# First 256 columns of two FFN weights loaded as f32 by the SyncE queue and rounded on chip, in a fused sparse-attention and GEGLU kernel

## The chip, the cores and the metric

One core of one Trainium2 chip. The metric is the device time of one execution in microseconds (us), the median of several runs. One run of the kernel before that took 1450.72 us is slow and left out. In the clock records of the traces here TensorE's granted clock is 1.00 or 0.50; each run's mean grant is given beside its time.

## The reference, cut to what matters

```python
def _attn_ref(q, k, v):                      # (4, 8, 768, 64)
    k_sum = k.reshape(B, H, nb, 32, D).max(axis=3)      # block maxima of keys
    v_sum = v.reshape(B, H, nb, 32, D).mean(axis=3)     # block means of values
    ...                                       # band of +-15 keys, and all block summaries
    return np.matmul(a, v_all)

def _moe_ref(x, w_gate, w_val, w_out, w_res):           # x (3072, 512), d_ff 1536
    g = x @ w_gate
    gelu = 0.5 * g * (1.0 + erf(g * inv_sqrt2))
    ffn_out = gelu * (x @ w_val) @ w_out
    res_gate = 1.0 / (1.0 + np.exp(-(x @ w_res)))
    return x + res_gate * ffn_out
```

All inputs are f32 in HBM; the kernel multiplies in bf16.

## The kernel before

The work is cut into eight units of 384 tokens. The attention of unit 0 has nothing to hide under; from then on the attention of unit n+1 lies between the FFN matmuls of unit n. All loads that turn f32 into bf16 go through the Pool queue, in this order: keys, queries, the twelve tiles of V, then both FFN weights in six chunks of 256 columns.

```python
v_loads(0, 0, 6)                   # V, 64 KB a tile as bf16, by the Pool queue
...                                # masks
v_loads(0, 6, NT)
...
for c in range(6):                 # 256 KB each as bf16, cast in flight
    sl = slice(c * 256, (c + 1) * 256)
    nc.gpsimd.dma_start(out=w_gate[:, :, sl], in_=wg_src[:, :, sl])
    nc.gpsimd.dma_start(out=w_val[:, :, sl], in_=wv_src[:, :, sl])
    if c == 4:
        q_sb[1] = load_q(1, QJ)
# then w_res, the rims of V, w_out, the next batch
```

The start of unit 0, where the change puts its load and its roundings (cuts marked):

```python
k_step(0, 3, ps_mm, "mm")          # last keys: turn, place, block maxima on VectorE
keep_warm(5)                       # matmuls for nothing, for TensorE's clock (see e3_warm)
...                                # queries, scores
nc.vector.tensor_copy(x[QT:BAND, 1:HT, :, 0:D], ...)        # vext copy 1
nc.vector.tensor_copy(x[QT:QT + WIN, 0:HT, :, 0:D], ...)    # vext copy 2
vsum_mm(0, vs, 0, 3)               # block means of V, tile by tile, on TensorE
...
vsum_mm(0, vs, 5, NT)              # needs V's last tile
nc.vector.tensor_copy(vblk[96:128, 0:H // 2, 0:D], ...)
nc.scalar.copy(vblk[96:128, H // 2:H, 0:D], ...)
nc.scalar.activation(gate1[:], bias_t[0:1, :], AF.Gelu)     # loads Gelu's table, 1.28 us
for hp in range(4):
    av_first(hp, st, ao[hp], 0, BAND)
...
for hp in range(4):
    av_first(hp, st, ao[hp], BAND, 128)
    av_end(hp, st, ao[hp])         # reciprocal and product on VectorE
...                                # turn x, then g and vv of the first unit
```

Names in the profile: `vext` is V with its rims, `vs` the block means of V as TensorE sums them and `vblk` the same as bf16; `ao` is attention's output, `xn` the same divided, `xT` it turned for the FFN; `g` and `vv` are the products with w_gate and w_val, `wp` the target of the warming matmuls, `w` the f32 tile w32.

The softmax here doesn't subtract the row's maximum and nothing guards it: scores larger than these inputs give would overflow.

## Time and profile before

| | kernel before |
|---|---|
| median of the timed runs, us | 260.91 (260.88 to 261.61) |
| the profiled run, us, and its span | 262.43, 260.5 |
| TensorE busy | 96% |
| V's last tile: issue, landing, us | 13.32, 16.2 |
| its sums on TensorE end, us | 17.76 |
| first reciprocal, first FFN matmul, us | 19.31, 21.33 |
| last chunk of w_val lands, us | 39.04 |

The lines of the page, the chain, the waits and the stretches stand in the prediction below. Here are TensorE's time line around V's last sums (start, length, operation, count), and V's last load.

```profile
16.06 1.70 PE L246 MATMUL vs<-vext,bmat 64*32 64x256 bf16 x14
17.69 0.95 PE L328 MATMUL ao<-vext,P 96*64 96x65 bf16 x48
...
19.78 0.82 PE L436 MATMUL wp<-warm 128*128 128x512 bf16 x3
```

```profile
L103 POOL DMA_DIRECT2D vext<-in_v_dram x1: 722/722/722, 13.3 to 13.3; - x1
...
DMA to landing us min/median/max: 2.9/2.9/2.9
```

No bracket stands behind the first two lines of TensorE, so it does not wait there: V's last tile is in place 1.2 us before its turn.

### The profile page before, as it was taken

Reading aid. Unit: us, or ns where it says so; the run is one execution under the profiler, and the core shown is the slowest. Engines: PE = TensorE matmul, PEld = TensorE weight load, DVE = VectorE, ACT = ScalarE, POOL = GpSimd, SP = SyncE. Lnnn points to the kernel's source line nnn. Section 1 sums busy time; section 2 is a strip of 40 time slices with the busy share of each in tenths; the row PEclk is TensorE's granted clock in tenths of the full one; section 3 lists DMA queues with packets and bytes.
Section 4 is the critical chain, followed back from the end, with each engine's and each line's share of the span. In section 5 each row is a group of like instructions: output and inputs, shape, how many; then the busy total and the mean of one; then the engine's idle time right before and its main releaser. Section 6 shows DMA issues by size and latency. Waiting matters only on the chain.

```text
span 260.5 us, 5798 instructions
## 1 busy us (share of the span) xinstructions
PE 251.3 (96%) x2294; PEld 138.1 (53%) x2294; DVE 156.1 (60%) x344; ACT 126.3 (48%) x210; POOL 104.5 (40%) x142
## 2 busy tenths in 40 slices
PE   6999889999999999999999999999999999999993
PEld 2565444555555565545654565545654565556543
DVE  5945562579657644577858544778666544854424
ACT  6685337557373435623383437443493338253320
POOL 8896345266080689045250898064530000000000
PEclk9999999999999999999999999999999999999999
DMA  5999999999962899949912999959903500230002
GB/s 82 177 123 174 197 214 203 196 118 193 79 121 47 145 161 123 143 117 156 133 40 56 179 131 137 113 128 164 154 4 85 140 0 3 48 137 0 0 20 103
DMA packets 98155, 29.61 MB, mean 114 GB/s; under 512 B 83368, under 2 KB 94960, under 8 KB 98016
## 3 DMA queue, kind: packets, MB, share of 16 engines
q0 software_dynamic: 68400, 14.96, 69.0%
q1 hardware_dynamic: 29728, 14.29, 25.0%
q8 instruction: 18, 0.29, 0.5%
q14 instruction: 9, 0.07, 0.1%
HBM read 29.36 MB, written 6.29 MB: 137 GB/s over the span
## 4 chain that ended last, share of the span: by engine, by line
PE 82%; DMA 11%; POOL 3%; ACT 1%; issue 1%; DVE 1%; POOLq 0%
PE f L404 23%; PE g L356 22%; PE vv L356 22%; PE r L394 8%; DMA w_val<-in_moe_w_val_dram 5%; DMA w_gate<-in_moe_w_gate_dram 3%; DMA q_sb<-in_q_dram 3%; PE ao L316 3%; PE s L280 2%; POOL vext L103 1%; PE f L428 1%; PE vs L254 1%; PE tp L205 1%; POOL w_val L190 1%; POOL w_gate L189 1%
## 5 line engine op out<-in xcount | busy, mean ns | idle before, releaser
L362 DVE TENSOR_TENSOR gvT<-ge,vv 128x384 bf16<-128x384 f32 x96 | 52.9, 553 | 53.4 <-PE vv L356 48.5
L361 ACT ACTIVATE ge<-g 128x384 f32<-128x384 f32 x96 | 46.9, 490 | 73.5 <-DVE gvT L362 43.5
L356 PE MATMUL vv<-xT,w_val 128*128 128x384 bf16 x384 | 78.8, 326 | 1.3 <-DMA w_val<-in_moe_w_val_dram 1.3
L356 PE MATMUL g<-xT,w_gate 128*128 128x384 bf16 x384 | 78.8, 326 | 0.2
L404 PE MATMUL f<-w_out,gvT 128*128 128x512 bf16 x276 | 64.9, 380 | 0.0
L356 PEld LDWEIGHTS <-w_val 128*128 128x128 bf16 x384 | 37.3, 98 | 27.0 <-DMA w_val<-in_moe_w_val_dram 2.8
L356 PEld LDWEIGHTS <-w_gate 128*128 128x128 bf16 x384 | 36.7, 98 | 26.1 <-issue 1.6
L404 PEld LDWEIGHTS <-gvT 128*128 128x128 bf16 x276 | 25.7, 98 | 29.4 <-issue 0.3
L103 POOL DMA_DIRECT2D vext<-in_v_dram x48 | 32.6, 716 | 13.2 <-DMA w_out<-in_moe_w_out_dram 4.8
L397 ACT ACTIVATE th<-r 128x512 f32<-128x512 f32 x24 | 13.6, 604 | 28.4 <-PE r L394 28.4
L266 POOL COPY vext<-vsum 32x1536 bf16<-32x1536 bf16 x12 | 17.1, 1463 | 23.2 <-DMA vsum<-vpart 23.2
L410 DVE SCALAR_TENSOR_TENSOR th<-th,f 128x512 f32<-128x512 f32 (+1 forms) x25 | 16.5, 661 | 15.7 <-PE f L404 15.4
L302 DVE TENSOR_TENSOR P<-P,maskt 128x768 bf16<-128x768 bf16 x28 | 16.2, 581 | 12.6 <-ACT P L298 8.0
L394 PE MATMUL r<-w_res,xT 128*128 128x512 bf16 x96 | 23.2, 380 | 0.0
L336 DVE TENSOR_TENSOR xn<-ao,rz 128x384 bf16<-128x384 f32 x32 | 17.8, 557 | 1.1
L413 DVE SCALAR_TENSOR_TENSOR o<-th,xn 128x512 f32<-128x512 f32 (+1 forms) x25 | 17.3, 691 | 0.9
L298 ACT ACTIVATE P<-s,bias_t 128x768 bf16<-128x768 f32 x17 | 15.3, 901 | 4.7 <-PE s L280 4.5
L117 POOL DMA_DIRECT2D k_nat<-in_k_dram x24 | 16.4, 746 | 0.9 <-DMA k_nat<-in_k_dram 0.5
L123 POOL DMA_DIRECT2D q_nat<-in_q_dram x18 | 15.9, 918 | 0.8 <-issue 0.7
L295 ACT ACTIVATE P<-s,bias_t 128x384 bf16<-128x384 f32 x30 | 15.7, 578 | 0.3 <-PE s L280 0.3
L212 DVE TENSOR_REDUCE ks<-kW 128x24 bf16<-128x768 bf16 x16 | 15.1, 944 | 0.1
L394 PEld LDWEIGHTS <-xT 128*128 128x128 bf16 x96 | 8.8, 98 | 9.9
(85 smaller groups left out, 167.9 us busy)
## 6 DMA issues: line engine op xcount, KB each, us to landing
out_dram<-o SPq DMA_DIRECT2D x23, 256.0 KB, 2.3
vext<-in_v_dram POOLq DMA_DIRECT2D x48, 64.0 KB, 6.4
q_nat<-in_q_dram POOLq DMA_DIRECT2D x18, 128.0 KB, 7.7
w_gate<-in_moe_w_gate_dram POOLq DMA_DIRECT2D x6, 256.0 KB, 9.4
w_val<-in_moe_w_val_dram POOLq DMA_DIRECT2D x6, 256.0 KB, 10.8
w_out<-in_moe_w_out_dram POOLq DMA_DIRECT2D x3, 512.0 KB, 11.7
k_nat<-in_k_dram POOLq DMA_DIRECT2D x24, 64.0 KB, 4.8
vext<-vext SPq DMA_DIRECT2D x6, 144.0 KB, 6.1
```

What stands on the lines that cost most here:

```text
L103: nc.gpsimd.dma_start(out=vext[b % 2][0:QT, t, :, 0:D], in_=v[b, :, t * QT:(t + 1) * QT, :].rearrange("h p d -> p h d"))
L117: nc.gpsimd.dma_start(out=k_nat[:, t].rearrange("p (h d) -> p h d", d=D), in_=k[b, :, t * QT:(t + 1) * QT, :].rearrange("h p d -> p h d"))
L266: eng.tensor_copy(vext[b % 2][96:128, lo:hi, :, 0:D], src)
L302: nc.vector.tensor_mul(Pf, Pf, maskt.unsqueeze(1).to_broadcast([128, 2 * HT, QT]))
L336: nc.vector.tensor_mul(xn, ao[:, :, :, 0:D], rz.to_broadcast([128, NSUB, 2, D]))
L356: nc.tensor.matmul(ps[:, 0:TU], w[:, ko, fo * 128:(fo + 1) * 128], st["xT"][:, ko, :], start=(ko == 0), stop=(ko == KO - 1), skip_group_ch ...
L361: nc.scalar.activation(ge[:], g[:, 0:TU], AF.Gelu)
L362: nc.vector.tensor_mul(gvT[:, fo, :], ge[:], vv[:, 0:TU])
L394: nc.tensor.matmul(r[:], st["xT"][:, ko, ss], w_res[:, ko, :], start=(ko == 0), stop=(ko == KO - 1))
L404: nc.tensor.matmul(st["f", sub][:], gvT[:, fo, ss], w_out[:, fo, :], start=(fo == 0), stop=(fo == FO - 1), skip_group_check=True)
L410: nc.vector.scalar_tensor_tensor(th[:, cs], th[:, cs], 1.0, f[:, 0:n], ALU.add, ALU.mult)
L413: nc.vector.scalar_tensor_tensor(o.rearrange("p (k d) -> p k d", d=128), th[:, cs].rearrange("p (k d) -> p k d", d=128), 0.5, x, ALU.mult, ...
```

## The change

The intent: the first chunks of both weights, with which every unit's FFN begins, no longer queue behind V on the Pool queue. They come by the SyncE queue, as f32 and without the cast that the Pool queue's loads do in flight, and VectorE and ScalarE round them in gaps of their own. The Pool queue has two chunks less to carry. Two memsets of one element make the load wait for VectorE to be through with the last keys' block maxima (in the trace after, the memsets start at 13.5 us and SyncE's first issue at 13.62).

```diff
+        w32 = qk.tile([128, 2, KO, 256], F32, tag="k_nat", name="w32")
...
-        for c in range(6):
+        for c in range(1, 6):
...
         k_step(0, 3, ps_mm, "mm")
+        for i in range(2):
+            nc.vector.memset(w32[0:1, i, 0, 0:1], 0.0)
+        nc.sync.dma_start(out=w32[:, 0], in_=wg_src[:, :, 0:256])
+        nc.sync.dma_start(out=w32[:, 1], in_=wv_src[:, :, 0:256])
         keep_warm(5)
...
+        nc.vector.tensor_copy(w_gate[:, :, 0:256], w32[:, 0])
         nc.scalar.activation(gate1[:], bias_t[0:1, :], AF.Gelu)
+        nc.scalar.copy(w_val[:, :, 0:256], w32[:, 1])
```

More of the change, by code (lines that the diff above doesn't have):

```diff
@@ L154, in own_keys @@
                                          ap=[rows.ap[0], [34, n]]), 1.0 / BLK)
+        w32 = qk.tile([128, 2, KO, 256], F32, tag="k_nat", name="w32")
+        wg_src = moe_w_gate.rearrange("(ko ki) f -> ki ko f", ki=128)
+        wv_src = moe_w_val.rearrange("(ko ki) f -> ki ko f", ki=128)
         nc.vector.memset(warm[:], 0.0)
@@ L182 @@
         nc.vector.memset(vext[1][0:QT, :, :, D + 1:VP], 0.0)
-        wg_src = moe_w_gate.rearrange("(ko ki) f -> ki ko f", ki=128)
-        wv_src = moe_w_val.rearrange("(ko ki) f -> ki ko f", ki=128)
-        for c in range(6):
+        for c in range(1, 6):
             sl = slice(c * 256, (c + 1) * 256)
```

## The prediction

> **What bounds the kernel now.** I read the page first, then the chain of waits in order of time, the waits of TensorE, the time line of each engine between 12 and 46 us, the transfers' landing times tile by tile, and the stretches' DMA rate. The page, by engine, by slice and by chain:
>
> ```profile
> PE 251.3 (96%) x2294; PEld 138.1 (53%) x2294; DVE 156.1 (60%) x344; ACT 126.3 (48%) x210; POOL 104.5 (40%) x142
> ...
> PE   6999889999999999999999999999999999999993
> ...
> PE 82%; DMA 11%; POOL 3%; ACT 1%; issue 1%; DVE 1%; POOLq 0%
> ```
>
> The reader is to see that TensorE is busy 96% of the span, so only some 9 us are not matmul time at all, and that no slice after the opening is empty. DMA owns 11% of the chain (28 us), but that is no gain of 28 us: TensorE works beneath nearly all of it. The chain in order of time says where those 11% lie:
>
> ```profile
> 3.15 7.21 DMA q_sb<-in_q_dram
> ...
> 17.51 8.75 DMA w_gate<-in_moe_w_gate_dram
> 26.54 12.49 DMA w_val<-in_moe_w_val_dram
> 39.09 0.82 PE vv L356 x4
> ```
>
> All before 39.1 us; from there on the chain is TensorE to the end. So the FFN weights' stream paces the first unit, and afterwards nothing but matmul count does. What the pacing costs is seen in TensorE's own waits and its time line:
>
> ```profile
> PE vv L356 <- DMA w_val<-in_moe_w_val_dram: 1.3, 2, 1.2
> PE tp L238 <- DMA q_sb<-in_q_dram: 0.8, 1, 0.8
> PE s L280 <- ACT qT L240: 0.3, 1, 0.3
> ...
> 31.90 0.82 PE L356 MATMUL vv<-xT,w_val 128*128 128x384 bf16 x4 [1.17 <-DMA w_val<-in_moe_w_val_dram]
> ...
> 36.09 0.36 PE L238 MATMUL tp<-ident,q_sb 96*64 96x96 bf16 x8 [0.76 <-DMA q_sb<-in_q_dram]
> ...
> 39.09 0.82 PE L356 MATMUL vv<-xT,w_val 128*128 128x384 bf16 x4 [0.18 <-DMA w_val<-in_moe_w_val_dram]
> ```
>
> Three waits, 1.17 + 0.76 + 0.18 = 2.1 us: about all that any better weight stream can return. The first FFN matmul (21.33 us) does not start late because of a weight: it follows ScalarE's copy of xT (20.80 us). Its partner on w_val waits 0.55 us of weight-load time for a landing at 21.6 us, which is at most 0.3 us more. Now the stream itself, by stretch (DMA share and GB/s as written are the last two numbers):
>
> ```profile
> 13.00:14.00 1.00, 1.00 (x19) 0.71 (x18) 0.93 (x5) 1.00 (x3) 1.00 (x3) 1.00 2.00 123
> 14.00:15.00 1.00, 1.00 (x18) 0.52 (x17) 0.97 (x2) 1.00 (x4) 1.00 (x3) 1.00 1.60 101
> 15.00:16.00 1.00, 1.00 (x18) 0.45 (x16) 0.75 (x1) 0.82 (x1) 1.00 (x1) 1.00 1.54 84
> 16.00:17.00 1.00, 1.00 (x19) 0.82 (x12) 0.00 (x0) 0.83 (x2) 1.00 (x3) 1.00 0.87 68
> 17.00:18.00 1.00, 1.00 (x26) 0.72 (x26) 0.31 (x1) 0.42 (x2) 1.00 (x2) 1.00 1.35 180
> ...
> 19.00:20.00 1.00, 1.00 (x49) 0.84 (x48) 0.66 (x2) 0.67 (x2) 1.00 (x3) 1.00 0.86 109
> ...
> 25.00:26.00 1.00, 1.00 (x8) 0.61 (x7) 0.67 (x2) 0.48 (x2) 0.76 (x1) 1.00 1.46 197
> ```
>
> From 22 to 36 us the stream holds 196 to 200 GB/s of bf16 written, i.e. 392 to 400 GB/s of f32 read, and I take that as its ceiling. Between 14 and 22 us it is below it, worst at 16 to 17 us: V has landed (last issue 13.3 us, 2.9 us to landing, so 16.2 us), while the first weight DMA, whose issue ends at 15.0 us, only begins to move. That hole is what the change aims at.
>
> [...] No run yet shows a SyncE load beside the Pool stream; the trace's 200 GB/s ceiling is what I hold it to. [...] the two first weight issues take 1.01 and 1.07 us beside VectorE's two copies into vext (13.62 to 15.75 us), the later ones 0.74 to 0.80 us. [...] No f32 copy within SBUF is in this trace. [...] 478 ns for 384 elements and 798 ns for 768, 0.83 ns each.
>
> **The change, part by part.**
> Removed: two 256 KB casting DMAs of the Pool queue, one of each weight. Everything behind them moves up two places. At the ceiling, 256 KB written takes 262 KB / 197 GB/s = 1.33 us, so the Pool stream would be 2.7 us ahead if the other queue cost it nothing.
> Added on DMA: the same f32 bytes on the SyncE queue, 2 x 524 KB. HBM reads stay at 29.36 MB. At 394 GB/s read they need 2.7 us of the ceiling as well. So the stream gains only as far as they fill time that was unused. Unused from 14.5 to 17.5 us, in bf16-equivalents: V's packets (128 B) run at up to 609 per half microsecond and weight packets (512 B) at 192, counted from the trace's records in half microseconds; scaled so, about 520 of the 1024 weight packets fit, 1.35 us. The dip of 19 to 22 us holds up to another 380 packets, 1.0 us, if it can be filled. Stream gain: 1.4 to 2.3 us.
> When they land: VectorE ends the last key's rims at 13.59 us, two memsets of 0.06 us follow, so SyncE issues at about 13.75 and 14.35 us (its issues last 0.34 to 0.62 us, and the stores' packets start some 0.75 us after an issue begins). Alone 1.35 us each; shared with V's tail and from 16.5 us with the Pool stream: w_gate lands at about 17 us, w_val at about 18.5 to 19.3 us (estimate).
> Added on VectorE: the rounding of 1024 elements a partition. [...] It sits behind the vblk cast (ends 18.12 us) and ahead of the first reciprocal (19.31 us), which waits 1.19 us for TensorE. It fits. The memsets' 0.13 us push the vext copies, behind which TensorE does not wait.
> Added on ScalarE: 1024 elements, 798 + 256 x 0.833 = 1.01 us. It sits behind the Gelu table's load and its dummy (end 19.68 us) and ahead of the first xT copy (20.80 us), idle for 1.12 us. It fits, with 0.1 us to spare, if w_val has landed by 19.7 us.
>
> What TensorE gets: the waits at 31.90, 36.09 and 39.09 us go if the stream leads by 1.2, 1.9 and 2.1 us. The next thing due, the first third of w_out (issued 33.0 us, 11.6 us to landing, needed at 44.69 us), has no slack now and must come 2 us earlier too. So TensorE's gain is the smaller of the stream's gain and some 2.2 us: 1.4 to 2.2, centre 1.8 us. TensorE is full from there, so it is carried to the end: 260.9 - 1.8 = 259.1 us, 0.7%.
>
> **The rivals.**
> A. The SyncE load lands late. Both roundings stand in in-order queues ahead of the softmax division and the xT copies, so each late microsecond delays the first FFN matmul by as much. For: before, w_val's first chunk landed 6.6 us after its issue at 15.0. Against: 1 us of margin on VectorE, the empty DMA time at 16 us, and a quicker queue. One microsecond late would leave the gain at about 1.2 us (the weights ahead would still have been the bound): 259.7 us. Two late: 260.6 us.
> B. The load delays V. V's last tiles land at 16.2 us, their sums need the last at about 17.4 us; small V packets that take turns with 1 KB packets could eat that 1.2 us. Then the vblk cast, attention and all behind slip by up to 1 us: 260 us.
> C. The bandwidth is only moved: the Pool stream loses to the SyncE queue what it gained, its dips stay, and the waits stay in another place. 260.9 us, no change.
> D. All waits go and the start is earlier by 0.3 us: 258.4 us.
>
> **Range and chances.** I give the main line 55%, A or B in part 25%, C 12%, D 8%. Range 258.3 to 260.7 us. The 2% mark is 5.2 us; the waits that can be removed are 2.4 us, and a loss of 5 us would need the load to land near 25 us. Faster 1%, within 2% 98%, slower 1%.
>
> **What will show it.** Right: no DMA idle above 0.3 us before the matmuls on w_val and the second q transposes; w_gate's f32 landing before 18.1 us and w_val's before 19.7 us; the first reciprocal still at 19.3 us, the first FFN matmul at 21.2 to 21.4 us; the stretch of 16 to 17 us above 150 GB/s; the matmuls behind the first unit some 1.8 us earlier, the rest of the trace shifted and unchanged. Wrong: VectorE or ScalarE idle on w32 (A); TensorE waiting for vext at 16 to 18 us (B); the last w_val still landing near 39 us (C).

## The result, and the profile after

The changed kernel took 263.65 us (262.72 to 264.48, four runs) beside 260.89 us of the kernel before: ratio 1.0101, 95% interval 1.0052 to 1.0149. Ratios are the mean time of one kernel's fast runs over that of the other's of the same rounds, so not quite the ratio of the medians. The runs fall into two pairs: 262.72 and 262.91 us at a mean clock of 0.992, 264.40 and 264.48 us at 0.987 and 0.986. The profile is of the run of 262.91 us. Its page:

```profile
span 261.0 us, 5804 instructions
...
PE 252.3 (97%) x2294; PEld 139.1 (53%) x2294; DVE 156.1 (60%) x347; ACT 127.3 (49%) x211; POOL 103.0 (39%) x140
...
PEclk9997999999999999999999999999999999999999
...
PE 89%; DMA 5%; POOL 2%; ACT 2%; DVE 1%; issue 0%; POOLq 0%
```

The reader is to see a contradiction: DMA's share of the chain fell from 11 to 5%, as was intended, TensorE is busier than before, and the run is longer. The one 7 in the row of the clock is the hint. TensorE's waits from 15 to 46 us and its time line give the rest:

```profile
PE vs L247 <- DMA vext<-in_v_dram: 1.5, 1, 1.5
PE s L281 <- ACT qT L241: 0.3, 1, 0.3
```

```profile
16.02 1.48 PE L247 MATMUL vs<-vext,bmat 64*32 64x256 bf16 x12
19.02 0.37 PE L247 MATMUL vs<-vext,bmat 64*32 64x256 bf16 x2 [1.51 <-DMA vext<-in_v_dram]
...
21.41 1.46 PE L437 MATMUL wp<-warm 128*128 128x512 bf16 x3
...
23.76 0.50 PE L357 MATMUL g<-xT,w_gate 128*128 128x384 bf16 x1
```

All waits for w_val and q_sb are gone. In their place stands a new one: the sums over V's last tile break off after 12 of 14 matmuls and wait 1.51 us. Then the three warming matmuls take 1.46 us in place of 0.82: TensorE runs at half clock. V's last load, issued at the same time as before, and the stretches around it (columns: length; busy us and instructions of PE, PEld, DVE, ACT, POOL; granted clock, DMA share, GB/s):

```profile
L103 POOL DMA_DIRECT2D vext<-in_v_dram x1: 722/722/722, 13.3 to 13.3; - x1
...
DMA to landing us min/median/max: 5.7/5.7/5.7
```

```profile
15.00:16.00 1.00, 1.00 (x18) 0.44 (x15) 0.73 (x1) 0.78 (x1) 1.00 (x1) 1.00 0.72 72
...
18.00:19.00 1.00, 0.00 (x0) 0.00 (x0) 0.00 (x0) 0.00 (x0) 1.00 (x3) 1.00 1.11 367
...
22.00:23.00 1.00, 1.00 (x7) 0.49 (x5) 0.96 (x3) 0.24 (x1) 0.33 (x1) 0.50 1.45 196
```

V's last tile lands 5.7 us after its issue, at 18.97 us, in place of 2.9. In the microsecond from 18 to 19 three engines do nothing at all, while the DMA engines move 367 GB/s. The granted clock is at 0.50 from 21.36 to 24.77 us, 3.41 us. What the DMA engines are busy with, in half a microsecond from 18.0 us (queue: packets, MB, share; q1 is SyncE's, q0 Pool's):

```profile
q1 hardware_dynamic: 179, 0.18, 103.4%
q0 software_dynamic: 17, 0.00, 6.0%
```

These 17 are the last of V's packets. The slowing began 3 us earlier: in the half microsecond from 15.0 us the Pool queue moved 402 packets in the kernel before, and here, with the load hardly begun:

```profile
q0 software_dynamic: 161, 0.02, 62.7%
q1 hardware_dynamic: 3, 0.00, 10.4%
```

In the half microsecond from 16.5 us it is 89 of Pool's to 111 of SyncE's. So V is held back while the load is in flight, but not simply by losing turns: from 15 to 16 us the DMA engines are busy less than before (the share is 0.72, and 1.54 in the prediction's table). What holds V's packets back is not shown. The roundings are innocent, as VectorE's and ScalarE's time lines show:

```profile
19.78 0.69 DVE L485 CAST w_gate<-w 128x1024 bf16<-128x1024 f32 x1
20.94 0.20 DVE L335 RECIPROCAL rz<-ao 128x6 f32<-128x6 f32 x1 [0.46 <-PE ao L329]
```

```profile
21.21 1.03 ACT L487 CAST w_val<-w 128x1024 bf16<-128x1024 f32 x1
23.23 0.48 ACT L344 COPY xT<-xp 128x384 bf16<-128x384 bf16 x1 [0.98 <-PE xp L342]
```

Behind each, its engine still waits for TensorE, 0.46 and 0.98 us. They fit into their gaps, only the gaps begin 1.6 us later.

### The profile page after: what moved, and what is told of

Its sections match the earlier page's. It is cut to its first block, busy times and chain, and to the rows that moved or that the text cites.

```text
span 261.0 us, 5804 instructions
## 1 busy us (share of the span) xinstructions
PE 252.3 (97%) x2294; PEld 139.1 (53%) x2294; DVE 156.1 (60%) x347; ACT 127.3 (49%) x211; POOL 103.0 (39%) x140
## 4 chain that ended last, share of the span: by engine, by line
PE 89%; DMA 5%; POOL 2%; ACT 2%; DVE 1%; issue 0%; POOLq 0%
PE g L357 24%; PE vv L357 24%; PE f L405 23%; PE r L395 8%; DMA q_sb<-in_q_dram 3%; PE ao L317 3%; PE s L281 2%; DMA vext<-in_v_dram 2%; POOL vext L103 1%; PE f L429 1%; PE vs L255 1%; PE wp L437 1%; PE xp L342 1%; PE tp L206 1%; PE ao L329 1%; POOL k_sb L88 1%
## 5 line engine op out<-in xcount | busy, mean ns | idle before, releaser
L411 DVE SCALAR_TENSOR_TENSOR th<-th,f 128x512 f32<-128x512 f32 (+1 forms) x25 | 16.5, 661 | 16.2 <-PE f L405 15.9
```

Of the source, the lines that this page charges most:

```text
L411: nc.vector.scalar_tensor_tensor(th[:, cs], th[:, cs], 1.0, f[:, 0:n], ALU.add, ALU.mult)
```

## The experiments

Theory 1: the load holds back V's last packets, TensorE stands idle for V's last tile, and the idle time makes its clock go down. Rival, theory 2: the two roundings, in order on busy engines, make the loss. Later a second question came up: why the gain on the other side is smaller than the profile promised. All ratios are to runs of the kernel before on the same chip in the same rounds.

| run | us, median | ratio (95%) | clock of the profiled run | V's last tile lands, us |
|---|---|---|---|---|
| changed kernel | 263.65 | 1.0101 (1.0052 to 1.0149) | 0.992 | 18.97 |
| e1_load_only | 263.94 | 1.0116 (1.0097 to 1.0134) | 0.987 | 18.87 |
| e2_no_load | 260.08 | 0.9978 (0.9965 to 0.9991) | 0.998 | 16.14 |
| e3_warm | 262.05 | 1.0055 (1.0038 to 1.0072) | 0.998 | 19.18 |
| e4_half | 262.83 | 1.0042 (1.0007 to 1.0078) | 0.992 | 18.94 |
| e5_mid | 266.16 | 1.0200 (1.0178 to 1.0222) | 0.984 | 16.64 |
| e8_start_half | 264.37 | 1.0098 (1.0064 to 1.0132) | 0.987 | 19.09 |
| e9_start_both | 262.65 | 1.0040 (1.0015 to 1.0065) | 0.991 | 18.15 |
| e10_tiny | 261.22 | 1.0012 (0.9996 to 1.0027) | 1.000 | 16.23 |
| e12_wide | 265.64 | 1.0171 (1.0139 to 1.0203) | 0.981 | 20.18 |
| c1_before | 261.12 | 0.9987 (0.9971 to 1.0003) | 0.997 | 17.10 |
| e11_hold | 260.72 | 0.9986 (0.9974 to 0.9998) | 0.998 | 16.40 |
| e13_swap | 260.64 | 0.9972 (0.9958 to 0.9986) | 1.000 | 16.18 |

### e1_load_only: the load without its use

```diff
 # against the changed kernel
-        for c in range(1, 6):
+        for c in range(6):
-        nc.vector.tensor_copy(w_gate[:, :, 0:256], w32[:, 0])
-        nc.scalar.copy(w_val[:, :, 0:256], w32[:, 1])
```

> The kernel before with the SyncE load of both f32 chunks added, but nothing read from it: all twelve Pool weight DMAs stay, no rounding. Theory 1 (the SyncE packets take turns with V's last small packets, V's last tile lands late, TensorE idles and its clock is then halved): V's last tile lands near 19.0 us instead of 16.2, TensorE idles 1.3 to 1.6 us before the last V sums, granted clock about 0.99, and the weight stream ends some 1 to 2 us later than before's 39.0 us; time 262 to 264.5 us. Theory 2 (the two roundings, in order on VectorE and ScalarE, make the loss): V lands at 16.2 us, clock 0.999, time below 261.7 us.

V's last tile at 18.87 us, TensorE idle for 1.44 us, clock down (mean grant 0.987), 263.94 us. There is no rounding in this kernel, so the loss does not need it; e2_no_load has the other half of the answer. The stream's end, 39.54 us, was only 0.5 us later than before's, less than expected.

### e2_no_load: the use without the load

```diff
 # against the changed kernel; the result is wrong on purpose
-        for i in range(2):
-            nc.vector.memset(w32[0:1, i, 0, 0:1], 0.0)
-        nc.sync.dma_start(out=w32[:, 0], in_=wg_src[:, :, 0:256])
-        nc.sync.dma_start(out=w32[:, 1], in_=wv_src[:, :, 0:256])
+        # near the start, while ScalarE is idle
+        nc.scalar.activation(w32.rearrange("p a k f -> p (a k f)"),
+                             warm[:, 0:1].to_broadcast([128, 2 * KO * 256]), AF.Copy)
```

> The changed kernel without the SyncE load; the f32 tile is filled with zeros by ScalarE at about 4.7 us, both roundings stay (wrong result on purpose). Theory 1: V's last tile lands at 16.2 us, no idle of TensorE before the last V sums, clock 0.999, first FFN matmul at 21.2 to 21.7 us, no wait for w_val or the second q; time 258 to 259.3 us. Theory 2: the roundings push the first reciprocal past 19.8 us or the first xT copy past 21.3 us, and time is 260 us or more.

The time line is as theory 1 has it: V at 16.14 us, first FFN matmul at 21.30, no wait for w_val or q_sb. (The time alone, 260.08 us, would have met theory 2's 260 us or more; its late reciprocal and late copy did not come.) (The zeros in the weights did not fail the comparison with the reference.) VectorE's rounding costs nothing:

```profile
18.12 0.69 DVE L483 CAST w_gate<-w 128x1024 bf16<-128x1024 f32 x1
19.28 0.20 DVE L337 RECIPROCAL rz<-ao 128x6 f32<-128x6 f32 x1 [0.46 <-PE ao L331]
```

But 260.08 us is above the 258 to 259.3 expected. With every weight's wait gone the kernel gains only 0.8 us on the median of the kernel before. As nothing is paid for the load here, I take that as the most this change could give; e13_swap, below, gets as far.

### e3_warm: TensorE busy while it waits

```diff
-        vsum_mm(0, vs, 5, NT)
+        vsum_mm(0, vs, 5, NT - 1)
+        keep_warm(7)
+        vsum_mm(0, vs, NT - 1, NT)
```

> The changed kernel with 7 warming matmuls ahead of the last V tile's sums, so that TensorE is busy while it waits for that tile. Theory 1 with the clock as the larger part: V's last tile still lands near 19 us, but the granted clock stays at 0.998 or more, the runs no longer fall into two groups, and time is 259.5 to 260.7 us. If the late tile alone makes the loss: time stays at 262 us or more.

V is as late as ever, 19.18 us, but the clock stays up, from 21.5 to 24.5 us too:

```profile
21.50:24.50 3.00, 2.86 (x42) 1.76 (x36) 2.54 (x8) 2.50 (x5) 1.54 (x2) 1.00 1.45 198
```

The time, 262.05 us, is 1.6 us better than the changed kernel, but though the clock held it just reaches the outcome named for a late tile alone (262 us or more). So the loss has two parts. Late V costs 262.05 - 260.08 = 2.0 us in this run, and the end of V's sums moves by as much (17.73 us in e2_no_load, 19.76 here). The clock costs the other 263.65 - 262.05 = 1.6 us. The split is rough: V's sums end 0.4 us later here than in the changed kernel (19.39 us), in part because V landed 0.2 us later.

### e5_mid: the load one microsecond later

```diff
         nc.vector.tensor_copy(x[QT:BAND, 1:HT, ...)         # vext copy 1
+        # both memsets and both SyncE loads moved to here
         nc.vector.tensor_copy(x[QT:QT + WIN, 0:HT, ...)     # vext copy 2
```

> The changed kernel with the two gating memsets and the SyncE load moved behind the first of the two copies into vext on VectorE, 1.05 us later. Theory 1: V's last tile lands by 16.8 us and the idle before its sums goes, at the price that the load now takes turns with the Pool weight packets and lands later (w_gate about 19 us, w_val 20 to 21.5 us), so the first reciprocal or the first xT copy is 0.5 to 1.5 us late; time 259.5 to 261.5 us. Theory 2: no better than the changed kernel, 262.7 us or more, because the roundings start later still.

V lands at 16.64 us as expected, and nothing waits for it. The time is the worst of all, far off the range that theory 1 gave; by its number it would speak for theory 2 (262.7 us or more). The trace tells why the roundings are late: now the load meets the Pool queue's weights, w_gate comes at 21.1 and w_val at 23.7 us, and both roundings stand in their queues ahead of what TensorE needs:

```profile
21.13 0.69 DVE L485 CAST w_gate<-w 128x1024 bf16<-128x1024 f32 x1 [2.88 <-DMA w<-in_moe_w_gate_dram]
21.85 0.20 DVE L335 RECIPROCAL rz<-ao 128x6 f32<-128x6 f32 x1
```

```profile
23.73 1.04 ACT L487 CAST w_val<-w 128x1024 bf16<-128x1024 f32 x1 [3.93 <-DMA w<-in_moe_w_val_dram]
24.80 0.86 ACT L344 COPY xT<-xp 128x384 bf16<-128x384 bf16 x2
```

TensorE stood idle 1.98 and 1.60 us and its clock was halved for 6.8 us. The prediction's rival A is real; in the changed kernel it does not occur, in part because V is late there (see below).

### c1_before: the kernel before once more

> The kernel before, unchanged, for a second look at its own spread. The theory to be tested: the profile that the prediction read was of a run (262.43 us with its profile, span 260.5) slower than the timed ones (260.3 to 261.84 us, spans 258.4 to 259.9 in the runs of the last batch), so the 2.1 us of waits for weights that it shows are more than the usual run has. Expected: time 260.9 us, span of the profile 258.4 to 259.9 us, and waits of TensorE for w_val and q_sb of 0.3 to 1.3 us in all in place of 2.1. Rival: the waits are 2 us again and the 1.5 us lie elsewhere.

```profile
PE f L404 <- DMA w_out<-in_moe_w_out_dram: 1.0, 1, 1.0
PE tp L238 <- DMA q_sb<-in_q_dram: 0.7, 1, 0.7
...
PE vv L356 <- DMA w_val<-in_moe_w_val_dram: 0.3, 1, 0.3
```

The waits for w_val and q_sb come to 1.0 us, inside the 0.3 to 1.3 expected; with w_out they come to 2.0 us again, as the rival had it. This profile, too, is of the slowest run of its kernel (261.63 us; the six lie between 260.83 and 261.63), and half of the waiting sits elsewhere: on w_out, for which the first profile did not show any. V's last tile landed at 17.10 us, 0.9 us later than in the first profile, with nothing on the SyncE queue, and still in time. A measure that leaves the single waits aside is the stretch from the first FFN matmul to the first of unit 1: 35.0 us in the first profile (21.33 to 56.37), 34.3 in this one, 33.5 in e10_tiny (whose weights travel as before), 32.4 in e2_no_load. So what there is to gain differs by 0.8 us between two runs of the same program, and by 1.6 us with e10_tiny, which adds a load of 8 KB alone; the profile that the prediction read had most of it.

### e4_half: only w_gate's chunk by SyncE

```diff
 # against the changed kernel: no load and no rounding for w_val, and
-        for c in range(1, 6):
+        for c in range(6):
+            if c:
                 nc.gpsimd.dma_start(out=w_gate[:, :, sl], ...)
             nc.gpsimd.dma_start(out=w_val[:, :, sl], ...)
```

> Only w_gate's first chunk goes by SyncE, at the same place as in the changed kernel; w_val's first chunk stays with the Pool queue, ahead of all its weights. If V's last packets are held back until the SyncE load is through: half the load, half the delay, V's last tile lands at 17.3 to 17.9 us, TensorE idles 0.2 to 0.7 us, the clock holds in most runs, time 260.3 to 261.6 us. If the delay were a fixed cost of a SyncE load being there: V at 19 us and 263 us or more.

V lands at 18.94 us in the profile, as late as with the whole load, so "half the load, half the delay" is wrong for that run. The six runs spread from 260.74 to 264.36 us, two of them with the clock at 1.0 (260.74 and 261.64), so V was probably earlier in those; only one trace was looked at.

### e8_start_half and e9_start_both: the load at the start of the program

```diff
 # e8: against e4_half; e9: against the changed kernel, with both loads
+        nc.sync.dma_start(out=w32[:, 0], in_=wg_src[:, :, 0:256])    # ahead of everything
-        ...                                                          # memsets, loads at the old place
```

> Only w_gate's first chunk by SyncE, issued ungated at the start of the program, where the DMA engines carry under 40 GB/s until 4 us. If the harm is only that the load meets V: the first keys land at most 0.7 us later than 6.5 us, V's last tile by 16.9 us, clock 0.998 or more, time 260.0 to 261.0 us, at best level with the run without a load (260.1 us). If a SyncE load harms wherever it is: keys and V late by over 1 us, time 261.5 us or more.

> Both chunks by SyncE at the start of the program, ungated, both roundings where they were. Twice the bytes into the same hole, so they overrun it by about 1.2 us: the first keys land near 7.5 to 8.5 us, V's last tile at 16.8 to 17.6 us, TensorE waits longer for the keys; time 260.3 to 262 us.

Both missed their ranges, e8_start_half by far: it met the other outcome named, a SyncE load that harms wherever it is. The keys are held back as V was: TensorE waits 2.89 us for the first keys with half the load and 2.44 us with all of it (1.09 in the kernel before), and the clock is halved for 6.8 and 3.4 us. Here is the line of e8_start_half, where 32 transposes take 1.49 us in place of 0.87:

```profile
8.21 1.49 PE L208 MATMUL tp<-ident,k_sb 96*64 96x96 bf16 x32 [2.89 <-DMA k_sb<-in_k_dram]
```

The half load ended by about 4 us and was the worse of the two. Why, is not settled; bytes alone do not explain it, nor do packets in flight: from 5.5 to 7 us, with the load over for 1.5 us, the Pool queue moved 182 packets, and 311 in the kernel before.

### e10_tiny and e12_wide: is it the queue, or what it carries?

```diff
 # against e1_load_only, in place of its two loads; e10_tiny:
+        nc.sync.dma_start(out=w32[:, 0, 0, 0:16], in_=wg_src[:, 0, 0:16])
 # e12_wide:
+        nc.sync.dma_start(out=w32[:, 0] as (128, 1024), in_=moe_w_gate[0:128, 0:1024])
+        nc.sync.dma_start(out=w32[:, 1] as (128, 1024), in_=moe_w_val[0:128, 0:1024])
```

> The kernel before with one tiny SyncE load at the same place (16 f32 of each of 128 rows, 8 KB in 64 B packets), nothing read from it. If merely starting the SyncE queue beside V's tail holds V back (the half load delayed V as much as the whole one): V's last tile lands later than 17.8 us, clock drops in some runs, time 262 us or more. If V is held back by the load's packets and bytes: V's last tile at 16.2 to 17.2 us as before, clock 0.997 or more, time 260.6 to 261.6 us.

> The kernel before with a SyncE load of the same 1 MB at the same place, but of full-length rows, 4 KB in a row and 256 pieces of it in place of 1024 of 1 KB; nothing read from it. If the bytes hold V back: V's last tile near 19 us and 263 to 264.5 us, as with the load in 1 KB pieces (263.94). If it is the turns that V's packets lose to each SyncE packet: V lands before 18 us with a quarter of the packets, or, if each turn is as long as its packet, as late as 19 us.

The tiny load costs nothing (V at 16.23 us, 1.0012), so the mere start of the SyncE queue is not the cause. The same megabyte in a quarter of the packets is worse than in e1_load_only (V at 20.18 us, 265.64 us), beyond both outcomes named. In the half microsecond from 16.0 us of e12_wide:

```profile
q1 hardware_dynamic: 47, 0.19, 100.1%
q0 software_dynamic: 6, 0.00, 2.3%
```

But a microsecond later, in the half microsecond from 17.0 us, it is 288 of Pool's to 31 of SyncE's. So no fixed share describes what V gets; that the load of longer packets was the worse one is all that the pair shows, and it reads other parts of the weights, too.

### e11_hold and e13_swap: keep the load apart from both neighbours

```diff
 # e11_hold: against e5_mid
         nc.vector.tensor_copy(x[QT:QT + WIN, 0:HT, ...)     # vext copy 2
+        gate3 = const.tile([128, 1], BF16, name="gate3")
+        nc.gpsimd.tensor_copy(gate3[QT:QT + WIN], x[QT:QT + WIN, HT - 1, 0, 0:1])
+        # the whole block of Pool weight DMAs moved to here
 # e13_swap: against e11_hold, the roundings exchanged
-        nc.vector.tensor_copy(w_gate[:, :, 0:256], w32[:, 0])
-        nc.scalar.copy(w_val[:, :, 0:256], w32[:, 1])
+        nc.scalar.copy(w_gate[:, :, 0:256], w32[:, 0])
...
             av_end(hp, st, ao[hp])
+            if hp == 1:
+                nc.vector.tensor_copy(w_val[:, :, 0:256], w32[:, 1])
```

> The changed kernel with the SyncE load moved behind the first vext copy, as in the run with V at 16.6 us, and the whole block of Pool weight DMAs held back until the second vext copy has ended (15.8 us), so that the load meets neither V nor the Pool weights. If the loss comes only from what the load meets: V at 16.3 to 16.9 us, w_gate rounded by 18.9 us and w_val by 20.7 us, clock 0.997 or more, first FFN matmul at 21.3 to 21.8 us, no wait for later weights, time 259.9 to 260.7 us, ahead of the kernel before. If the SyncE load itself is slow here: w_gate lands after 19 us, first reciprocal after 20 us, time 261.5 us or more.

> The held version with the roundings exchanged: ScalarE rounds w_gate (landing near 19.4 us, in the gap between the Gelu table's load and the first xT copy), VectorE rounds w_val (landing near 20.8 us) after the second pair of heads instead of ahead of the first reciprocal. If the 1.1 us that the held version loses at the first reciprocal are all that is left of the harm: first reciprocal at 19.3 us again, first FFN matmul at 21.3 to 21.8 us, time 259.9 to 260.5 us. If the start does not count because the weight stream is again the bound: 260.7 us as the held version, with waits of TensorE for w_val or q_sb.

Between V and the weights there is a hole, and e11_hold makes it wide enough. From 16.5 to 18.5 us the SyncE queue has the DMA engines to itself:

```profile
DMA packets 661, 0.66 MB, mean 331 GB/s; under 512 B 15, under 2 KB 661, under 8 KB 661
...
q1 hardware_dynamic: 661, 0.66, 99.5%
```

V lands at 16.40 us, the clock stays at 0.998, the time is 260.72 us, just ahead of the kernel before. But w_gate is there only at 19.4 us, 4.5 us after its issue, and its rounding ends at 20.4 us, 1.5 us past what was expected; the first reciprocal comes at 20.45 us. This part is as foreseen for a load that is slow by itself, though the time of 261.5 us foreseen with it was not reached. e13_swap mends that: the piece that lands first is rounded by the engine whose gap is later.

```profile
19.21 0.20 DVE L322 RECIPROCAL rz<-ao 128x6 f32<-128x6 f32 x1 [1.19 <-PE ao L316]
...
20.61 0.68 DVE L497 CAST w_val<-w 128x1024 bf16<-128x1024 f32 x1
```

First reciprocal at 19.21 us, first FFN matmul at 21.23 (22.39 in e11_hold), 0.9972 of the kernel before: 0.3% ahead of it, as much as e2_no_load, which had no load at all. That it also beats e11_hold is not clear of noise, as their intervals overlap. Its median, 260.64 us, is above the range expected, but that batch's runs of the kernel before were slower as well (261.55 us).

## Why the prediction was wrong

By its own steps:

- **The waits at 31.90, 36.09 and 39.09 us go: right.** None is left in the profile after.
- **The stream gains 1.4 to 2.3 us: about right.** The last w_val chunk lands at 36.14 us in place of 39.04, 2.9 us earlier than in the profile that was read, and 1.5 us earlier than in c1_before (37.64).
- **The roundings fit: right in length, lucky in time.** ScalarE's took 1.03 us for the 1.01 worked out from its copies in the trace before (478 ns for 384 elements, 798 ns for 768). VectorE's took 0.69 us; that it would fit was the estimate, as that trace has no f32 copy within SBUF to read a length from. But the load was slower than "alone 1.35 us each": its last packet moved at 20.42 us, past the 19.7 us that the prediction had set for w_val and 6.3 us after the issue of w_val's load at 14.13 us. The "quicker queue" shows in the trace before for SyncE's stores alone (256 KB, 2.3 us from issue to landing in the median, beside 9.4 us for the Pool queue's chunks of w_gate). ScalarE's rounding found its data ready because late V had moved its gap to 21.2 us. With V in time, it would have waited some 0.7 us (an estimate, from the 19.68 us at which the dummy Gelu ended before). The Pool's DMA issue beside VectorE's rounding took 1.10 us (at 19.68 us in the changed kernel) against 0.75 to 0.79 for those just before it; in e11_hold the rounding beside a Pool issue took 1.00 us in place of 0.69.
- **V ("small V packets that take turns with 1 KB packets could eat that 1.2 us"): this is the step that failed.** It was a rival with "up to 1 us" and 260 us. The thought was of turns: V would need somewhat longer. The packets of both queues do mix (from 16.5 to 17 us, in order of their starts, the 200 records change queue 102 times), but regular turns are not shown. Instead V fell from 402 to 161 packets in half a microsecond when the load had moved 3, and trickled out beside it, 17 to 179 at the end. V's last tile was late by 2.8 us, of which the margin took 1.2; TensorE's wait of 1.51 us is what was left, and e3_warm against e2_no_load prices the delay at 2.0 us.
- **TensorE's clock: not in the prediction at all.** The kernel is full of warming matmuls, put there for the clock, yet the rival counted only the slip. The idle time was paid twice: TensorE waited 1.51 us, and 2.3 us after it took up work again at 19.02 us its granted clock fell to 0.50. e3_warm, which fills the wait, keeps the clock at 1.00, and prices it at 1.6 us. A gap of 1.17 us in the kernel before (until 31.90 us) had no such effect: the clock records of that profile stay at 1.00 up to 260 us. In the clock records the half clock lasts 3.41 us here, 6.8 us in e1_load_only and 10.2 us in e12_wide (mean grants 0.992, 0.987 and 0.981). Nearly the same idle time, 1.51 and 1.44 us, cost 3.41 us of half clock here and twice that in e1_load_only; why, no run shows. 3.41 us at half clock lose at most 1.7 us (an estimate, half of 3.41), and the two pairs of runs of the changed kernel are 1.6 us apart; no trace of the slower pair was kept.
- **The gain of 1.8 us: the mechanism was right, the size was not.** e2_no_load gains 0.8 us on the median. The 2.1 us were read from a profile of a run that was itself 1.5 us above the median, which stood in the times all along. That runs differ so much in these waits is shown; what makes them differ is not.

The 0.8, 2.0 and 1.6 us are steps along one row of medians (kernel before, e2_no_load, e3_warm, changed kernel), so that they add up proves nothing. The traces of e2_no_load and of the changed kernel give a check: V's sums end 1.66 us later (17.73 and 19.39 us), the first FFN matmul starts 2.46 us later (21.30 and 23.76), unit 1's first 2.93 us later (53.67 and 56.60), and from there to the end both take 204.5 us within 0.1. So late V is 1.7 us of it and the 3.41 us of half clock 1.3; the two runs' times differ by 2.8 us. As e1_load_only loses as much without roundings and e2_no_load loses nothing with them, no cause of that size is left over. Open is how a SyncE load in flight holds back the Pool queue: why V slowed before the load had moved more than 3 packets, why half a load delays V as much as a whole one in e4_half's trace, and why half a load at the start holds up the keys longer than a whole one.

## What to carry to other kernels

A load on a second queue is not hidden because its own consumer does not wait for it: ask which transfers are in flight beside it and which of them is due first, and do not count on an even share: V's last tile, with 1.2 us of margin, came 2.8 us late. Idle time on TensorE must be priced with the clock that it may cost: 1.51 us of waiting were followed here by 3.41 us at a granted clock of 0.50, worth 1.6 us. And before a wait in a profile is counted as a gain, compare the profiled run's time with the median of the timed ones.
